# A modelled deadline for VectorE's background work, and 1024-wide products, in an attention and state-space kernel

## The chip, the cores and the metric

One core of a Trainium2 chip. The time is device microseconds (us) of the whole kernel, in the median of repeated executions. PE is the matmul engine (PEld its weight loads), ScalarE (ACT in the records) does exponentials, VectorE (DVE) does everything elementwise here, and SP issues DMA. The times of one kernel on one chip spread by 0.08% to 0.25%, mostly about 1 us.

## The reference, cut to what matters

The kernel computes two things from the same `x` (2048 x 1024) and mixes them with a gate:

```python
a = state_space(x)     # Bu = x @ B_bar; h[t] = Lam_bar * h[t-1] + Bu[t] (complex, 1024 states); y = 2 Re(h @ C) + x * Dskip
b = attention(x)       # 32 heads of 32, 2048 x 2048 scores per head, softmax, @ wo
g = sigmoid((x * gate_w).sum(-1))
out = g * a + (1 - g) * b
```

The softmax needs 32 x 2048 x 2048 exponentials, which is 1,024 tiles of 128 x 1024. Everything else is arranged around them.

## The kernel before: the parts that matter

The program is a fixed order of 512 *bursts*. A burst puts score matmuls for two tiles into PSUM (4 x 2 `qk` pairs), has both tiles exponentiated, multiplies exponentials of earlier bursts, mostly two or three ago, with V (`pv`, in "quarters"), and adds about four *dense* matmuls of 512 columns from a list: projections (`proj`, `vproj`), state inputs (`u`), output maps (`c`), the output projection (`out`). Dense matmuls all use one PSUM bank, so VectorE must evacuate the bank before the next dense group starts.

The two exponentials of a burst normally both run on ScalarE. In 52 listed bursts VectorE makes half of the first tile with a polynomial, and ScalarE only the other half:

```python
def dve_bursts():
    out = []
    for lo, hi, m in ((172, 188, 4), (204, 254, 4), (296, 332, 4), (400, 508, 4)):
        out += [B for B in range(lo, hi) if B % m == 1 and B != 457]
    return out
DVB = set(dve_bursts())
...
    # in exp(B, z, s)
    if z == 0 and B in DVB:
        self.dve_exp(B, s, p)       # ScalarE 128x512, VectorE 128x512 in one PSUM pass and four SBUF passes
    else:
        self.act(lambda e: e.activation(self.tile[p], ps[:, 2 * s:2 * s + 2, :], ACT.Exp, scale=SCALE), ...)
```

VectorE's queue is filled at build time. Between evacuations the builder places *background*: tables, folded maps, and for each of 32 state tiles the rotation, scan and rotation back. The old rule used one constant period per burst:

```python
PERIOD = 1.81 ; DPERIOD = 1.40          # us per burst, without and with VectorE's help
...
early = 0.1 + 0.1 * len(tail) + (0.2 if used < base else 0.0)
limit = t0 + (period - early if ended is not None else period + (0.3 if p + 1 in DVB else PE_HEAD))
while not self.dx and (self.bg or self.bg2):
    ...
    if c > 0 and st + c > limit:
        break
    src.pop(0)[1]()                     # the op goes into VectorE's queue here
```

The background of a state tile (real and imaginary part, each 128 x 512 bf16) had eight narrow products:

```python
tt(0.335, t[0], ure, er, ALU.mult, ...)      # and three more, then two adds into fp32
...                                          # two scans
tt(0.335, t[0], hre, er, ALU.mult, ...)      # and three more, then two adds
```

Of the kernel before, what the change touches and what calls it, by code (L numbers as in the profile page):

```python
# [12 lines left out]
ALU = mybir.AluOpType  # L13
# [912 lines left out]
QUNITS = 8  # L926
BURSTS = 8
NBURST = GROUPS * QUNITS * BURSTS
PERIOD = 1.81
PE_HEAD = 0.86  # L930
MM_PER_PERIOD = 4
DPERIOD = 1.40
EXP_A = 16713.9646930418
EXP_B = 4936176.0
EXP_C2 = 189883.03836007958
# [11 lines left out]
DVB = set(dve_bursts())  # L947
# [17 lines left out]
class FastPath:  # L965
# [86 lines left out]
    def dve(self, fn, r, w, name=""):  # L1052
        return self.S.op("dve", fn, reads=r, writes=w, name=name)
# [271 lines left out]
    def table_ops(self, j):  # L1325

        EF, Et, prod = self.EF, self.Et, self.fold.rearrange("p (k a b) -> p k a b", k=4, a=32)
        lo = [EF[:, r, 16 * j:16 * (j + 1)].unsqueeze(1).to_broadcast([128, 32, 16]) for r in range(2)]
        hi = [EF[:, r, 128 + 32 * j:160 + 32 * j].unsqueeze(2).to_broadcast([128, 32, 16]) for r in range(2)]
        first = ["m_a0", "m_a1", "m_a2", "m_k", "m_h", "m_y", "m_s"] if j == 0 else []  # L1330
        over = [("pt", 12 + j // 2), ("pt", 16 + j // 2)]
        ops = []
        for k, (x, y) in enumerate(((0, 0), (1, 1), (0, 1), (1, 0))):
            ops.append((0.62, lambda k=k, x=x, y=y: self.dve(lambda e: e.tensor_tensor(prod[:, k], hi[x], lo[y], ALU.mult), self.EFtok, ["gp%d" % k] + (first if k == 0 else []))))
        for r, op in ((0, ALU.subtract), (1, ALU.add)):
            out = Et[:, r, j, :].rearrange("p (a b) -> p a b", a=32)
            ops.append((0.62, lambda r=r, op=op, out=out: self.dve(lambda e: e.tensor_tensor(out, prod[:, 2 * r], prod[:, 2 * r + 1], op), ["gp%d" % (2 * r), "gp%d" % (2 * r + 1)],
                                                                   [("Et", j)] + (over if r == 0 else []) if r == 0 else [("Et", j)])))
        ops.append((0.0, lambda: self.tabled.append(j)))
        return ops  # L1340

    def item_ops(self, j, ch, n):
        dve, ub, tq, ut, ht = self.dve, self.ub, self.tq, self.ut, self.ht
        b = self.hp_of[ch]
        hp = self.hpb[b]
        er, ei = self.Et[:, 0, j, :], self.Et[:, 1, j, :]
        k = self.ub_of(n)
        ure, uim = ub[k][:, 0, :], ub[k][:, 1, :]
        u0, u1, Et = ("ub", k, 0), ("ub", k, 1), ("Et", j)
        t = [tq[:, i, :] for i in range(4)]  # L1350
        ops = []

        def tt(c, o, a, b, op, r, w):
            ops.append((c, lambda: dve(lambda e: e.tensor_tensor(o, a, b, op), r, w)))  # L1354
        tt(0.335, t[0], ure, er, ALU.mult, [u0, Et], [("tq", 0)])
        tt(0.335, t[1], uim, ei, ALU.mult, [u1, Et], [("tq", 1)])
        tt(0.335, t[2], uim, er, ALU.mult, [u1, Et], [("tq", 2)])
        tt(0.335, t[3], ure, ei, ALU.mult, [u0, Et], [("tq", 3)])
        tt(0.6, ut[:, 0, :], t[0], t[1], ALU.add, [("tq", 0), ("tq", 1)], [("ut", 0)])
        tt(0.6, ut[:, 1, :], t[2], t[3], ALU.subtract, [("tq", 2), ("tq", 3)], [("ut", 1)])  # L1360
        rr = self.pf[:, self.RR, j:j + 1].to_broadcast([128, 512])
        for ri in range(2):
            ops.append((1.29, lambda ri=ri: dve(lambda e: e.tensor_tensor_scan(ht[:, ri, :], rr, ut[:, ri, :], self.init[:, ri, j:j + 1], ALU.mult, ALU.add),  # L1363
                                                [("ut", ri), "init", ("pf", self.RR)], [("ht", ri)])))
        if ch < 3:
            ops.append((0.13, lambda: dve(lambda e: e.tensor_copy(self.hl[:, :, j], ht[:, :, 511]), [("ht", 0), ("ht", 1)], [("hl", j)])))
        hre, him = ht[:, 0, :], ht[:, 1, :]
        tt(0.335, t[0], hre, er, ALU.mult, [("ht", 0), Et], [("tq", 0)])
        tt(0.335, t[1], him, ei, ALU.mult, [("ht", 1), Et], [("tq", 1)])
        tt(0.335, t[2], hre, ei, ALU.mult, [("ht", 0), Et], [("tq", 2)])  # L1370
        tt(0.335, t[3], him, er, ALU.mult, [("ht", 1), Et], [("tq", 3)])
        hw = ["warm"] if ch == 0 and j == 0 else []
        if ch == 2 and j >= 4:
            hw = self.x_toks(0)
        if b == 1 and j == 0:
            hw = ["fX", "fY", "m_c"] + self.EFtok + ["gp%d" % i for i in range(4)]
        tt(0.335, hp[:, 0, j, :], t[0], t[1], ALU.subtract, [("tq", 0), ("tq", 1)], [("hp", b, j, 0)] + hw)
        tt(0.335, hp[:, 1, j, :], t[2], t[3], ALU.add, [("tq", 2), ("tq", 3)], [("hp", b, j, 1)] + hw)
        if j == 7 and ch < 3:
            ops.append((0.0, self.carry))  # L1380
        return ops
# [159 lines left out]
    def plan(self):  # L1541
# [3 lines left out]
        used = {}  # L1545
# [35 lines left out]
        for b in sorted(range(RING), key=lambda b: when.get(b, b)):  # L1581
            p = when.get(b, b)
            ok = [(end, t) for t, end in pairs if free[t] < p and used[b] < end and not (end == NBURST and used[b] >= RING + t[0] // 2)]
            assert ok, (b, p)

            near = [(end, t) for end, t in ok if end - used[b] <= 1]
            end, t = min(near) if near else max(ok)
            free[t] = used[b]
            self.pt_at[b] = t
        self.ring_at, k, x = {}, 2 * RING, 0  # L1590
        for B in range(RING, NBURST):
            for z in range(2):
# [141 lines left out]
    def build(self):  # L1734
# [50 lines left out]
        wo1 = last = False  # L1785
        nal = nc = 0
        self.c_end = 0
        tnext = 0.0
        nq = 0
        log = self.log = []  # L1790
        for p in range(first, NBURST):
# [1 line left out]
            assert not proj[g] or (g == 0 and p < 32)  # L1793
            self.p = p
            second = self.burst(p)
            t0 = tnext
            period = DPERIOD if p in DVB else PERIOD
            tnext = t0 + period
            if p in DVB:
                self.dve_t = max(self.dve_t, t0 + 0.35) + 0.70  # L1800
            nq += len(self.quarters[p])
            ends = nq % 32 == 0 and self.quarters[p]
            ntail = 0
            if p % 2 and not ends:
                ntail = 1 if p in DVB else 2 if p + 2 in DVB else 0
            head, tail = self.split_pv(p, ntail)
            self.pv(head)
            second()
            if ends:
                self.normalize(nq // 32 - 1)  # L1810
                self.dve_t = max(self.dve_t, t0 + PE_HEAD) + 0.75
            if p >= C_LOADS and p % 4 == 0 and nc < 8:
                self.ld_c(nc)
                nc += 1
# [23 lines left out]
            if g >= 6 and not cs and self.c_left[3] == 0 and nal < 8 and p > self.c_end:  # L1838
                self.ld_a(nal)
                nal += 1  # L1840
            used = 0.0
            quota = 3 if p in DVB else 5 if p + 1 in DVB and not 442 <= p < 459 and (cur is None or cur.left >= 8) else MM_PER_PERIOD
            base = quota
            ended = None
            while used < quota:
# [31 lines left out]
                wt, f = cur.pieces.pop(0)  # L1877
                f()
                used += wt
                cur.left -= wt  # L1880
                if not cur.pieces:
                    ended = cur
# [1 line left out]
                elif used >= quota and cur.left <= 1 and quota == base:  # L1884
                    quota += 1
            self.pv(tail)
            log.append((p, ended.tag if ended else (cur.tag if cur else None), used, round(self.dve_t - t0, 2), len(self.bg) + len(self.bg2)))
            early = 0.1 + 0.1 * len(tail) + (0.2 if used < base else 0.0)
            limit = t0 + (period - early if ended is not None else period + (0.3 if p + 1 in DVB else PE_HEAD))
            while self.dx:  # L1890
                c, fn = self.dx[0]
                st = max(self.dve_t, t0)
                if st + c > limit:
                    break
                self.dx.pop(0)
                fn()
                self.dve_t = st + c
            while not self.dx and (self.bg or self.bg2):
                src = self.bg if self.bg and (self.bg[0][2] in self.tabled or not self.bg2) else self.bg2
                if not src:  # L1900
                    break
                c = src[0][0]
                st = max(self.dve_t, t0 + 0.3)
                if c > 0 and st + c > limit:
                    break
                src.pop(0)[1]()
                if c > 0:
                    self.dve_t = st + c
            if getattr(self, "seen_items", 0) != self.items_done:
                self.seen_items = self.items_done  # L1910
                self.item_p = p
            if ended is not None:
                ended.evac()
                self.dve_t = max(self.dve_t, t0 + period - early + 0.1) + 0.70 + ended.extra
        self.log = log
        assert not outs and cur is None and nq == 4 * NBURST - 8
        self.tail()

    def tail(self):

# [178 lines left out]
```

## Time and profile before

| | before |
|---|---|
| median of 4 runs | 940.23 us (939.22 to 940.47) |
| ScalarE / PE / VectorE busy | 98% / 99% / 72% |
| first exponential ends / last ends / end of span | 11.00 / 929.70 / 939.17 us |

The first part of the profile page, busy time of each engine with its share of the span and its instructions:

```profile
span 939.2 us, 33706 instructions
...
PE 925.4 (99%) x15316; PEld 520.3 (55%) x15316; DVE 674.1 (72%) x1357; ACT 923.2 (98%) x1034; POOL 10.0 (1%) x39
```

Two engines look full. The chain of waits that ended last, by engine, even names PE first:

```profile
PE 61%; ACT 36%; SPq 1%; DMA 1%; issue 0%; DVE 0%; DVEq 0%
```

The Trainium skill, "Perfetto Trace Analysis", section "Identifying the Most-Contended Engine", warns that a matmul engine's busy share is no good measure of how close it is to its limit, because matmuls are pipelined, while for ScalarE and VectorE the occupancy is a fair one. This trace agrees: PE's 99% includes 57.6 us that its weight loads stood waiting for ScalarE, hidden under matmuls whose ends are modelled. The list of waits (who waited for whom, us in total, times, longest):

```profile
PEld f_ps L1635 <- ACT f_pt L1651: 57.6, 143, 0.6
DVE f_ub L1452 <- PE f_ps L1446: 40.4, 47, 3.0
DVE f_Ag L1488 <- PE f_ps L1475: 18.4, 32, 1.8
```

The second line shows what the change is after: VectorE stood idle in front of 47 of the 48 evacuations of state inputs that go to `ub` (16 more go to another tile). The old rule let the background run only to 0.1 to 0.5 us before the burst's booked end.

The table by stretches of time (start and end, length, then busy us and instructions of each engine, PE's granted clock, DMA share, GB/s):

```profile
core 0: us, PE busy (x) PEld busy (x) DVE busy (x) ACT busy (x) POOL busy (x), PEclk, DMA share, GB/s
100.00:200.00 100.00, 99.92 (x1662) 54.42 (x1659) 86.69 (x174) 100.00 (x111) 1.68 (x6) 1.00 0.37 68
300.00:400.00 100.00, 99.90 (x1665) 56.82 (x1664) 69.67 (x141) 100.00 (x114) 1.51 (x6) 1.00 0.12 30
927.50:930.50 3.00, 3.00 (x39) 1.65 (x38) 1.80 (x4) 2.20 (x3) 0.00 (x0) 0.50 0.11 37
```

ScalarE is busy 100.00 of 100 us, but PE is at 99.9 too, so this table alone does not say which of them sets the time. ScalarE's busy time cannot show small stalls, though, because consecutive records overlap. So I took the *ends* of consecutive ScalarE instructions from the trace: 903 of 1,033 are 0.915 to 0.920 us apart, and the end of a half-wide one follows after 0.490 us. What these distances have beyond 0.9165 or 0.4905 us, summed from the end of the first exponential to the end of the last, is called the **stall sum** below; three small instructions in between are taken out with their own time. Before: 2.99 us of 918.7.

The groups of the narrow products (count, then shortest/median/longest duration in ns, first and last start):

```profile
L1354 DVE TENSOR_TENSOR f_tq<-f_ht,f_Et x128: 398/418/426, 63.6 to 725.8; 128x512 bf16<-128x512 bf16 x128
L1354 DVE TENSOR_TENSOR f_tq<-f_ub,f_Et x96: 415/418/424, 53.7 to 718.0; 128x512 bf16<-128x512 bf16 x96
```

They last 0.418 us but follow each other every 0.334 us in the trace: the record of one overlaps the next.

### The profile page before, as it was taken

The numbers are of one execution on the slowest core, as the hardware profiler recorded it, in microseconds if no ns is written. First come the engines' busy times: TensorE is split into PE (matmuls) and PEld (weight loads), VectorE is DVE, ScalarE is ACT, GpSimd is POOL, SyncE is SP. The second block draws the span as 40 slices with busy tenths as digits, with TensorE's granted clock in tenths as the row PEclk, the third lists the DMA queues.
The fourth block names the chain that finished last, engine by engine and source line by source line (L and its number), as shares of the span: only waits on it lengthen the run. The fifth ranks groups of instructions, "written<-read, shape, count | busy, mean of one in ns | idle before, by whom it ended". The sixth has DMA issues, their size and how long they took to land.

```text
span 939.2 us, 33706 instructions
## 1 busy us (share of the span) xinstructions
PE 925.4 (99%) x15316; PEld 520.3 (55%) x15316; DVE 674.1 (72%) x1357; ACT 923.2 (98%) x1034; POOL 10.0 (1%) x39
## 2 busy tenths in 40 slices
PE   8999999999999999999999999999999999999996
PEld 4555645565555565555655755544655556555553
DVE  2688888888888766657688766568838466676775
ACT  6999999999999999999999999999999999999996
POOL 2000000000000000000000000000000000000000
PEclk9999999999999999999999999999999999999998
DMA  9659433310133002121023301142201212233412
GB/s 202 104 93 146 76 56 80 74 31 27 34 66 89 30 6 52 41 72 31 19 42 61 75 16 42 42 94 53 53 5 40 73 52 79 80 87 122 115 62 74
DMA packets 157076, 60.90 MB, mean 65 GB/s; under 512 B 145664, under 2 KB 145664, under 8 KB 156928
## 3 DMA queue, kind: packets, MB, share of 16 engines
q1 hardware_dynamic: 154768, 58.16, 28.0%
q8 instruction: 121, 1.98, 0.9%
q10 hardware_dynamic: 2160, 0.53, 0.3%
q14 instruction: 27, 0.22, 0.1%
HBM read 16.79 MB, written 12.58 MB: 31 GB/s over the span
## 4 chain that ended last, share of the span: by engine, by line
PE 61%; ACT 36%; SPq 1%; DMA 1%; issue 0%; DVE 0%; DVEq 0%
ACT f_pt L1651 33%; PE f_ps L1703 17%; PE f_ps L1635 13%; PE f_ps L1446 9%; PE f_ps L1475 9%; PE f_ps L1416 8%; PE f_ps L1434 4%; ACT f_ub L1671 1%; SPq L1068 1%; ACT f_cT_re L1651 1%; DMA f_xT<-in_A_x_dram 1%; ACT f_Et L1651 1%; ACT f_cT_im L1651 1%; PE f_ps L1481 1%; ACT f_OT L1651 0%
## 5 line engine op out<-in xcount | busy, mean ns | idle before, releaser
L1651 ACT ACTIVATE f_pt<-f_ps 128x1024 bf16<-128x1024 f32 x892 | 834.0, 1277 | 0.6 <-PE f_ps L1635 0.6
L1703 PEld LDWEIGHTS f_ps<-f_V,f_pt 128*128 128x128 bf16 x7136 | 228.4, 96 | 115.9 <-issue 94.1
L1703 PE MATMUL f_ps<-f_V,f_pt 128*128 128x33 bf16 x7136 | 279.6, 178 | 0.0
L1635 PE MATMUL f_ps<-f_Q,f_K 32*128 32x256 bf16 x4096 | 230.3, 273 | 3.8 <-ACT f_cT_re L1651 1.2
L1635 PEld LDWEIGHTS f_ps<-f_Q,f_K 32*128 32x128 bf16 x4096 | 80.3, 92 | 158.5 <-issue 73.0
L1446 PE MATMUL f_ps<-f_xT,f_wb 128*128 128x512 bf16 x512 | 131.0, 377 | 0.3
L1416 PE MATMUL f_ps<-f_xT,f_wb 128*128 128x512 bf16 x464 | 119.0, 378 | 0.0
L1363 DVE TENSOR_TENSOR_SCAN f_ht<-f_pf,f_init,f_ut 128x512 bf16<-128x512 f32 x64 | 80.4, 1272 | 0.0
L1475 PE MATMUL f_ps<-f_cT_re,f_hp 128*128 128x512 bf16 x192 | 72.6, 378 | 0.1
L1475 PE MATMUL f_ps<-f_cT_im,f_hp 128*128 128x512 bf16 x192 | 72.6, 378 | 0.0
L1506 PE MATMUL f_ps<-f_wb,f_OT 128*128 128x512 bf16 x252 | 65.7, 379 | 0.1
L1452 DVE CAST f_ub<-f_ps 128x512 bf16<-128x512 f32 x48 | 33.2, 692 | 40.4 <-PE f_ps L1446 40.4
L1434 PE MATMUL f_ps<-f_wb,f_xT 128*128 128x128 bf16 x896 | 59.2, 219 | 0.0
L1446 PEld LDWEIGHTS f_ps<-f_xT,f_wb 128*128 128x128 bf16 x512 | 40.4, 96 | 32.0
L1416 PEld LDWEIGHTS f_ps<-f_xT,f_wb 128*128 128x128 bf16 x464 | 36.3, 96 | 28.0
L1434 PEld LDWEIGHTS f_ps<-f_wb,f_xT 128*128 128x128 bf16 x896 | 50.4, 97 | 0.0
L1672 DVE TENSOR_SCALAR f_ut<-f_ps 128x512 int32<-128x512 f32 x26 | 18.0, 692 | 39.9 <-PE f_ps L1635 39.9
L1354 DVE TENSOR_TENSOR f_tq<-f_ht,f_Et 128x512 bf16<-128x512 bf16 x128 | 45.9, 417 | 0.0
L1354 DVE TENSOR_TENSOR f_ut<-f_tq 128x512 f32<-128x512 bf16 x64 | 42.1, 683 | 0.0
L1488 DVE TENSOR_SCALAR f_Ag<-f_ps,f_gcol 128x512 f32<-128x512 f32 x32 | 24.0, 751 | 18.4 <-PE f_ps L1475 18.4
L1354 DVE TENSOR_TENSOR f_tq<-f_ub,f_Et 128x512 bf16<-128x512 bf16 x96 | 34.6, 417 | 0.0
L1423 DVE CAST f_Q<-f_ps 128x512 bf16<-128x512 f32 x30 | 20.8, 692 | 15.9 <-PE f_ps L1416 15.8
(152 smaller groups left out, 853.6 us busy)
## 6 DMA issues: line engine op xcount, KB each, us to landing
ag_scratch<-f_Ag SPq DMA_DIRECT2D x32, 256.0 KB, 2.5
f_hp<-ag_scratch SPq DMA_DIRECT2D x32, 256.0 KB, 2.9
f_wb<-in_B_wqkv_dram SPq DMA_DIRECT2D x21, 256.0 KB, 4.3
out_dram<-f_xT SPq DMA_DIRECT2D x16, 256.0 KB, 2.1
f_wb<-in_B_wo_dram SPq DMA_DIRECT2D x1, 1024.0 KB, 5.2
f_OT<-f_On SPq DMA_TRANSPOSE x63, 2.3
f_wb<-in_B_wo_dram SPq DMA_DIRECT2D x1, 768.0 KB
f_wb<-in_B_wqkv_dram ACTq DMA_DIRECT2D x2, 256.0 KB, 4.2
```

The costliest lines, as they stand in the source:

```text
L1354: ops.append((c, lambda: dve(lambda e: e.tensor_tensor(o, a, b, op), r, w)))
L1363: ops.append((1.29, lambda ri=ri: dve(lambda e: e.tensor_tensor_scan(ht[:, ri, :], rr, ut[:, ri, :], self.init[:, ri, j:j + 1], ALU.mult, ...
L1416: mms.append((1, lambda e, f, l, a=a: e.matmul(ps[:, bank, :], w[:, g % 2, part, a, :], xT[:, a, 512 * ch:512 * (ch + 1)], start=f, stop=l ...
L1434: m = e.matmul(ps[:, bank, 128 * q:128 * (q + 1)], xT[:, a, 128 * kt:128 * (kt + 1)], w[:, g % 2, 2, a, :], start=(a == 0), stop=(a == 7))
L1446: mms.append((1, lambda e, f, l, a=a: e.matmul(ps[:, 7, :], bT[:, n % 2, ri, a, :], xT[:, a, 512 * ch:512 * (ch + 1)], start=f, stop=l), [ ...
L1452: self.dve(lambda e: e.tensor_copy(self.ub[k][:, ri, :], ps[:, 7, :]), [("bank", 7)], [("ub", k, ri)] + over, "evac_u")
L1475: mms.append((1, lambda e, f, l, j=j, ri=ri: e.matmul(ps[:, 7, :], hp[:, ri, j, cols], cT[ri][:, j, 512 * cb:512 * (cb + 1)], start=f, sto ...
L1488: self.dve(lambda e: e.tensor_scalar(a, ps[:, 7, :], self.gcol[:, 0, tt:tt + 1], None, ALU.mult), [("bank", 7), "g0"], [at], "evac_c")
L1506: mms.append((1, lambda e, f, l, j=j: e.matmul(ps[:, 7, :], OT[:, j, 256 * qb + 128 * r:256 * qb + 128 * (r + 1)], wo[j][0][:, 512 * cb:51 ...
L1635: m = e.matmul(ps[:, 2 * sl[z] + h % 2, 256 * kl:256 * (kl + 1)], K[32 * h:32 * h + 32, g % 2, 128 * kt:128 * (kt + 1)], Q[32 * h:32 * h + ...
L1651: self.act(lambda e: e.activation(self.tile[p], ps[:, 2 * s:2 * s + 2, :], ACT.Exp, scale=SCALE), [("S", s)], [("pt", p)], "exp")
L1703: m = e.matmul(ps[:, 6, o:o + 33], self.tile[p][:, h2, 256 * kl + 128 * qt:256 * kl + 128 * (qt + 1)], V[:, g % 2, 2 * i + kl, h, :], star ...
```

## The change

Its intent: fill VectorE's idle time before evacuations without making them late, and make the background shorter. The diff, cut to its core:

```diff
-PERIOD = 1.81
-PE_HEAD = 0.86
+ACT_2 = 0.9165          # full exponential, also ACT_1 = 0.49, lags, and
+QK_PE = 0.34            # PE's time for scores; PV_PE = 0.101 per quarter, MM_PE = 0.2157 per dense matmul
...
-        tt(0.335, t[0], ure, er, ALU.mult, [u0, Et], [("tq", 0)])
-        tt(0.335, t[1], uim, ei, ALU.mult, [u1, Et], [("tq", 1)])
-        tt(0.335, t[2], uim, er, ALU.mult, [u1, Et], [("tq", 2)])
-        tt(0.335, t[3], ure, ei, ALU.mult, [u0, Et], [("tq", 3)])
+        E2, E2r = self.Et[:, :, j, :], self.Et[:, ::-1, j, :]       # both table halves; the same in reversed order
+        tt(0.602, tq[:, 0:2, :], ub[k], E2, ALU.mult, [u0, u1, Et], [("tq", 0)])
+        tt(0.602, tq[:, 2:4, :], ub[k], E2r, ALU.mult, [u0, u1, Et], [("tq", 2)])
...                                                  (the same for ht)
-        tnext = 0.0
+        self.T = self.act_t = self.evac_t = 0.0
...
-                ntail = 1 if p in DVB else 2 if p + 2 in DVB else 0
+            ntail = 2 if p % 2 and not ends else 0      # PV quarters behind the dense matmuls in odd bursts
...
+            a0 = max(self.act_t, T + QK_LAG) + (ACT_1 if isd else ACT_2)
+            self.act_t = a0 + ACT_2
+            self.T = max(ta, tp)                        # the next burst starts when ScalarE frees a tile and PE is done
+            if ended is not None:                       # a dense group ended: leave room for its evacuation
+                cost = 0.608 if ended.tag in ("proj", "vproj", "u") else 0.668
+                nxt_dense = self.T + QK_PE + PV_PE * len(self.quarters.get(p + 1, ()))
+                self.fill(max(ready, nxt_dense - cost - 0.15))
+            else:
+                self.fill(self.T + (QK_LAG if p + 1 in DVB else 1.0))
```

The 512 bursts, their exponentials, the list of VectorE's half exponentials and the matmuls stay.

More of the change, by code (lines that the diff above doesn't have):

```diff
@@ L928 @@
 NBURST = GROUPS * QUNITS * BURSTS
-PERIOD = 1.81
-PE_HEAD = 0.86
+ACT_2 = 0.9165
+ACT_1 = 0.49
+ACT_LAG = 0.466
+QK_LAG = 0.449
+QK_PE = 0.34
+PV_PE = 0.101
+MM_PE = 0.2157
 MM_PER_PERIOD = 4
-DPERIOD = 1.40
 EXP_A = 16713.9646930418
@@ L1331, in table_ops @@
         over = [("pt", 12 + j // 2), ("pt", 16 + j // 2)]
+        after = 1 + max(self.tile_end.get(t, 0) for t in (12 + j // 2, 16 + j // 2))
         ops = []
         for k, (x, y) in enumerate(((0, 0), (1, 1), (0, 1), (1, 0))):
-            ops.append((0.62, lambda k=k, x=x, y=y: self.dve(lambda e: e.tensor_tensor(prod[:, k], hi[x], lo[y], ALU.mult), self.EFtok, ["gp%d" % k] + (first if k == 0 else []))))
+            ops.append((0.6, lambda k=k, x=x, y=y: self.dve(lambda e: e.tensor_tensor(prod[:, k], hi[x], lo[y], ALU.mult), self.EFtok, ["gp%d" % k] + (first if k == 0 else []))))
         for r, op in ((0, ALU.subtract), (1, ALU.add)):
             out = Et[:, r, j, :].rearrange("p (a b) -> p a b", a=32)
-            ops.append((0.62, lambda r=r, op=op, out=out: self.dve(lambda e: e.tensor_tensor(out, prod[:, 2 * r], prod[:, 2 * r + 1], op), ["gp%d" % (2 * r), "gp%d" % (2 * r + 1)],
-                                                                   [("Et", j)] + (over if r == 0 else []) if r == 0 else [("Et", j)])))
+            ops.append((0.6, lambda r=r, op=op, out=out: self.dve(lambda e: e.tensor_tensor(out, prod[:, 2 * r], prod[:, 2 * r + 1], op), ["gp%d" % (2 * r), "gp%d" % (2 * r + 1)],
+                                                                   [("Et", j)] + (over if r == 0 else []) if r == 0 else [("Et", j)]), after))
         ops.append((0.0, lambda: self.tabled.append(j)))
@@ L1354, in tt @@
             ops.append((c, lambda: dve(lambda e: e.tensor_tensor(o, a, b, op), r, w)))
-        tt(0.335, t[0], ure, er, ALU.mult, [u0, Et], [("tq", 0)])
-        tt(0.335, t[1], uim, ei, ALU.mult, [u1, Et], [("tq", 1)])
-        tt(0.335, t[2], uim, er, ALU.mult, [u1, Et], [("tq", 2)])
-        tt(0.335, t[3], ure, ei, ALU.mult, [u0, Et], [("tq", 3)])
-        tt(0.6, ut[:, 0, :], t[0], t[1], ALU.add, [("tq", 0), ("tq", 1)], [("ut", 0)])
-        tt(0.6, ut[:, 1, :], t[2], t[3], ALU.subtract, [("tq", 2), ("tq", 3)], [("ut", 1)])
+        E2, E2r = self.Et[:, :, j, :], self.Et[:, ::-1, j, :]
+        tt(0.602, tq[:, 0:2, :], ub[k], E2, ALU.mult, [u0, u1, Et], [("tq", 0)])
+        tt(0.602, tq[:, 2:4, :], ub[k], E2r, ALU.mult, [u0, u1, Et], [("tq", 2)])
+        tt(0.6, ut[:, 0, :], t[0], t[1], ALU.add, [("tq", 0)], [("ut", 0)])
+        tt(0.6, ut[:, 1, :], t[3], t[2], ALU.subtract, [("tq", 2)], [("ut", 1)])
         rr = self.pf[:, self.RR, j:j + 1].to_broadcast([128, 512])
         for ri in range(2):
-            ops.append((1.29, lambda ri=ri: dve(lambda e: e.tensor_tensor_scan(ht[:, ri, :], rr, ut[:, ri, :], self.init[:, ri, j:j + 1], ALU.mult, ALU.add),
+            ops.append((1.192, lambda ri=ri: dve(lambda e: e.tensor_tensor_scan(ht[:, ri, :], rr, ut[:, ri, :], self.init[:, ri, j:j + 1], ALU.mult, ALU.add),
                                                 [("ut", ri), "init", ("pf", self.RR)], [("ht", ri)])))
         if ch < 3:
-            ops.append((0.13, lambda: dve(lambda e: e.tensor_copy(self.hl[:, :, j], ht[:, :, 511]), [("ht", 0), ("ht", 1)], [("hl", j)])))
-        hre, him = ht[:, 0, :], ht[:, 1, :]
-        tt(0.335, t[0], hre, er, ALU.mult, [("ht", 0), Et], [("tq", 0)])
-        tt(0.335, t[1], him, ei, ALU.mult, [("ht", 1), Et], [("tq", 1)])
-        tt(0.335, t[2], hre, ei, ALU.mult, [("ht", 0), Et], [("tq", 2)])
-        tt(0.335, t[3], him, er, ALU.mult, [("ht", 1), Et], [("tq", 3)])
+            ops.append((0.19, lambda: dve(lambda e: e.tensor_copy(self.hl[:, :, j], ht[:, :, 511]), [("ht", 0), ("ht", 1)], [("hl", j)])))
+        tt(0.602, tq[:, 0:2, :], ht[:], E2, ALU.mult, [("ht", 0), ("ht", 1), Et], [("tq", 0)])
+        tt(0.602, tq[:, 2:4, :], ht[:], E2r, ALU.mult, [("ht", 0), ("ht", 1), Et], [("tq", 2)])
         hw = ["warm"] if ch == 0 and j == 0 else []
@@ L1376, in item_ops @@
             hw = ["fX", "fY", "m_c"] + self.EFtok + ["gp%d" % i for i in range(4)]
-        tt(0.335, hp[:, 0, j, :], t[0], t[1], ALU.subtract, [("tq", 0), ("tq", 1)], [("hp", b, j, 0)] + hw)
-        tt(0.335, hp[:, 1, j, :], t[2], t[3], ALU.add, [("tq", 2), ("tq", 3)], [("hp", b, j, 1)] + hw)
+        tt(0.335, hp[:, 0, j, :], t[0], t[1], ALU.subtract, [("tq", 0)], [("hp", b, j, 0)] + hw)
+        tt(0.335, hp[:, 1, j, :], t[2], t[3], ALU.add, [("tq", 2)], [("hp", b, j, 1)] + hw)
         if j == 7 and ch < 3:
@@ L1589, in plan @@
             self.pt_at[b] = t
+        self.tile_end = {t: e for pr, e in free.items() for t in pr}
         self.ring_at, k, x = {}, 2 * RING, 0
@@ L1795, in build @@
             second = self.burst(p)
-            t0 = tnext
-            period = DPERIOD if p in DVB else PERIOD
-            tnext = t0 + period
-            if p in DVB:
-                self.dve_t = max(self.dve_t, t0 + 0.35) + 0.70
+            T = self.T
+            isd = p in DVB
+            a0 = max(self.act_t, T + QK_LAG) + (ACT_1 if isd else ACT_2)
+            self.act_t = a0 + ACT_2
+            ta = a0 + ACT_LAG
+            if isd:
+                self.dve_t = max(self.dve_t, T + QK_LAG) + 0.608
+                ta = max(ta, self.dve_t + 0.19)
             nq += len(self.quarters[p])
             ends = nq % 32 == 0 and self.quarters[p]
-            ntail = 0
-            if p % 2 and not ends:
-                ntail = 1 if p in DVB else 2 if p + 2 in DVB else 0
+            ntail = 2 if p % 2 and not ends else 0
+            if isd:
+                ntail = min(ntail, 1)
             head, tail = self.split_pv(p, ntail)
@@ L1808, in build @@
             second()
+            pe = T + QK_PE + PV_PE * len(head)
             if ends:
+                rn = pe + 0.35
+                self.fill(rn)
                 self.normalize(nq // 32 - 1)
-                self.dve_t = max(self.dve_t, t0 + PE_HEAD) + 0.75
+                self.dve_t = max(self.dve_t, rn) + 0.6
             if p >= C_LOADS and p % 4 == 0 and nc < 8:
@@ L1841, in build @@
             used = 0.0
+            if cur is None:
+                pe = max(pe, self.evac_t)
             quota = 3 if p in DVB else 5 if p + 1 in DVB and not 442 <= p < 459 and (cur is None or cur.left >= 8) else MM_PER_PERIOD
@@ L1879, in build @@
                 used += wt
+                pe += MM_PE if wt else 0.055
                 cur.left -= wt
@@ L1886, in build @@
             self.pv(tail)
-            log.append((p, ended.tag if ended else (cur.tag if cur else None), used, round(self.dve_t - t0, 2), len(self.bg) + len(self.bg2)))
-            early = 0.1 + 0.1 * len(tail) + (0.2 if used < base else 0.0)
-            limit = t0 + (period - early if ended is not None else period + (0.3 if p + 1 in DVB else PE_HEAD))
-            while self.dx:
-                c, fn = self.dx[0]
-                st = max(self.dve_t, t0)
-                if st + c > limit:
-                    break
-                self.dx.pop(0)
-                fn()
-                self.dve_t = st + c
-            while not self.dx and (self.bg or self.bg2):
-                src = self.bg if self.bg and (self.bg[0][2] in self.tabled or not self.bg2) else self.bg2
-                if not src:
-                    break
-                c = src[0][0]
-                st = max(self.dve_t, t0 + 0.3)
-                if c > 0 and st + c > limit:
-                    break
-                src.pop(0)[1]()
-                if c > 0:
-                    self.dve_t = st + c
+            ready = pe + 0.2
+            tp = pe + PV_PE * len(tail) + 0.1
+            self.T = max(ta, tp)
+            log.append((p, ended.tag if ended else (cur.tag if cur else None), used, round(self.T - T, 3), round(self.dve_t - T, 2), len(self.bg) + len(self.bg2), round(self.T, 2), round(tp - T, 3)))
+            if ended is not None:
[4 more added lines that the diff above has]
+                self.fill(self.T + (QK_LAG if p + 1 in DVB else 1.0))
             if getattr(self, "seen_items", 0) != self.items_done:
@@ L1913, in build @@
                 ended.evac()
-                self.dve_t = max(self.dve_t, t0 + period - early + 0.1) + 0.70 + ended.extra
+                st = max(self.dve_t, ready)
+                self.evac_t = st + cost + 0.13
+                self.dve_t = st + cost + ended.extra
         self.log = log
@@ L1917, in build, with fill @@
         self.tail()
+    def fill(self, limit):
+        while True:
+            for src in (self.dx, self.bg, self.bg2):
+                if not src:
+                    continue
+                if src is self.bg:
+                    n = src[0][2]
+                    if n < 8 and n not in self.tabled or n >= 8 and len(self.folded) < 16:
+                        continue
+                if src is self.bg2 and len(src[0]) > 2 and self.p < src[0][2]:
+                    continue
+                c = src[0][0]
+                if c == 0 or self.dve_t + c <= limit:
+                    src.pop(0)[1]()
+                    self.dve_t += c
+                    break
+            else:
+                return
     def tail(self):
```

## The prediction

> **What bounds the kernel now.** ScalarE's exponentials. The table by stretches of time shows ScalarE busy 100.00 of every 100 us from 50 us to 900 us. In the trace, the ends of consecutive 128x1024 exponentials are 0.916 to 0.918 us apart in 850 of 1,033 cases, and 0.490 us after a half-wide one. 972 full and 52 half instructions make 972 x 0.9165 + 52 x 0.4905 = 916.3 us. The first exponential ends at 11.0 us and the last at 929.7 us, so 918.7 us hold 916.3 us of work: the stalls of ScalarE in the whole middle are about 2.4 us. They are crumbs of 0.02 to 0.13 us: at 60 to 118 us (bursts where PE itself needs over 1.83 us) and around 413-430, 575-612 and 757-793 us (bursts where VectorE takes half an exponential). In front stand 11 us of head, behind 9.5 us of tail. It agrees with the Trainium skill, "ScalarE: Activation LUTs", which states one element per cycle and lane whatever the function (0.833 ns per element): 1024 of them are 0.853 us of the measured 0.917.
>
> PE's 99% includes modelled ends; in the list of waits its score matmuls wait 57.6 us for ScalarE. VectorE is 72% busy.
>
> **What the change does.** (1) Eight 512-wide bf16 products per state tile become four 1024-wide ones. Back-to-back ends in the trace: 0.334 us for 512 wide bf16, 0.601 us for the same count with fp32 output, which is about 0.068 us fixed plus 0.52 or 1.04 ns per element. So a 1024-wide bf16 product is an estimated 0.60 us against 0.668 us for two; 128 pairs give 8.7 us, provided the reversed order of the two table halves keeps the fast mode. The Trainium skill, "VectorE: DVE Perf Modes", asks for 16-bit and step one, which the inner dimension keeps; this case's 0.334 against 0.601 us agrees with its factor of two. (2) A new rule fills VectorE's queue with background up to a modelled deadline. Its durations equal the trace's (1.19 scan, 0.60, 0.9165). (3) Two of a burst's PV quarters move behind its dense matmuls in nearly every odd burst, which gives evacuations 0.2 us more. (4) State projections and output chunks come some bursts earlier or later. The 512 bursts, the exponentials, VectorE's share of them, PE's total work, head and tail stay.
>
> **On the critical path:** almost nothing. VectorE's 8.7 us were not on it. Only stalls can change: at best -2.4 us, realistically -0.5 to -1. Against that, VectorE runs closer to its deadlines; a late evacuation delays the next dense group, and past some tenths of a us ScalarE stalls.
>
> **Prediction:** 939.3 us, 8 in 10 between 937.5 and 942.0. Faster by over 2%: 0.01; within 2%: 0.97; slower by over 2%: 0.02.
>
> **What would show it.** VectorE's busy time falls from 674 to about 665 us; the product line shows 64+48+16 instructions of 128x1024, spaced 0.60 us; ScalarE still 100 of 100 us in each stretch; its end-to-end spacing still 0.917 us; summed stalls between first and last exponential between 1.5 and 4 us; the last exponential ends near 928-931 us, with the same 9.5 us behind it.
>
> **What would make it wrong.** A reversed outer step that loses the fast mode (about 1.13 us per op, 64 ops, +34 us of VectorE and a model that no longer holds, so repeated late evacuations); background put in front of evacuations in many bursts; or moved PV quarters holding tiles that the next exponential overwrites.

## The result, and the profile after

| | before | after |
|---|---|---|
| median of 4 runs each | 940.23 us | 940.29 us (939.77 to 940.92) |
| ratio, 95% interval | | 1.0003, 0.9986 to 1.002: the same |
| stall sum | 2.99 us | 3.07 us |
| first exponential's end to last one's | 918.70 us | 918.78 us |

Ratios here are the mean time of one kernel's fast runs over the mean of the other's in the same rounds, so not quite the ratio of the quoted medians.

The first part of the page, and the list of waits, after:

```profile
span 938.2 us, 33573 instructions
...
PE 923.3 (98%) x15316; PEld 532.7 (57%) x15316; DVE 659.5 (70%) x1229; ACT 923.0 (98%) x1034; POOL 11.3 (1%) x39
```

```profile
PEld f_ps L1637 <- ACT f_pt L1653: 42.8, 104, 0.6
DVE f_ub L1453 <- PE f_ps L1447: 24.1, 25, 3.0
DVE f_Ag L1489 <- PE f_ps L1476: 39.5, 29, 6.6
```

The change does on VectorE what it was meant to do: 128 instructions fewer, 14.6 us less busy, and idle time in front of 25 of 48 evacuations of state inputs into `ub` instead of 47. The idle time did not vanish, though, but moved to other evacuations: in front of those of the output maps (`Ag`) it grew from 18.4 to 39.5 us. The new order did this, not the shorter products, since it is 49.0 us in `order_only` below and 19.6 us in `wide_only`. The groups of the wide products:

```profile
L1359 DVE TENSOR_TENSOR f_tq<-f_ht,f_Et x64: 679/684/692, 59.2 to 720.8; 128x1024 bf16<-128x1024 bf16 x64
L1359 DVE TENSOR_TENSOR f_tq<-f_ub,f_Et x48: 678/684/693, 52.4 to 714.9; 128x1024 bf16<-128x1024 bf16 x48
```

All lie within 0.678 to 0.693 us, so the half of them that read the table with a reversed outer step run as fast as the others. One directly behind another, they end 0.600 to 0.607 us apart (47 cases, median 0.602), against twice 0.334.

And nothing of it reaches the time. The table by stretches:

```profile
core 0: us, PE busy (x) PEld busy (x) DVE busy (x) ACT busy (x) POOL busy (x), PEclk, DMA share, GB/s
100.00:200.00 100.00, 100.00 (x1635) 55.91 (x1631) 91.00 (x170) 100.00 (x110) 2.04 (x6) 1.00 0.38 70
300.00:400.00 100.00, 99.98 (x1670) 58.45 (x1669) 52.17 (x96) 100.00 (x114) 0.00 (x0) 1.00 0.12 30
927.50:930.50 3.00, 2.66 (x59) 1.82 (x53) 2.21 (x8) 2.42 (x3) 0.00 (x0) 1.00 0.25 92
```

From 300 to 400 us VectorE has 17.5 us less to do (the second chunk's state tiles are written by 287 us instead of 327), and ScalarE is at 100.00 of 100 as before.

A trap lies in the last row. The profiled span fell by 1.0 us, from 939.2 to 938.2. But from 927.5 to 930.5 us the run before was granted half the PE clock (0.50), the run after the full one, and the tail behind the last exponential took 9.47 us in one and 8.24 us in the other. The stretch between first and last exponential is equal to 0.1 us. Of the 1.23 us between the tails, 0.96 had arisen by the start of the first reciprocal behind the last exponential (1.42 us after its end in one run, 0.46 in the other). The medians of the runs agree with the stretch, not with the span; the profiled execution of before (940.91 us) is not among the four runs of the table and lies above all of them.

The stall sum stayed because one part fell and another rose. In the stretch 560 to 620 us it fell from 0.81 to about 0.5 us. From 40 to 60 us, where there had been less than 0.03 us, there are now 0.68 us, most of it one stall. ScalarE's timeline there, first before, then after (start, duration, instruction; in brackets idle time and what ended it):

```profile
43.30 2.23 ACT L1651 ACTIVATE f_pt<-f_ps 128x1024 bf16<-128x1024 f32 x2
45.20 1.25 ACT L1651 ACTIVATE f_cT_re<-f_ps 128x1024 bf16<-128x1024 f32 x1
```

```profile
43.30 2.13 ACT L1653 ACTIVATE f_pt<-f_ps 128x1024 bf16<-128x1024 f32 x2
45.78 1.02 ACT L1653 ACTIVATE f_cT_re<-f_ps 128x1024 bf16<-128x1024 f32 x1 [0.34 <-PE f_ps L1637]
```

What led to it, from the same timeline of after, VectorE and PE:

```profile
42.42 0.55 DVE L1283 SCALAR_TENSOR_TENSOR f_OT<-f_OT 128x384 f32<-128x384 f32 x1
43.01 0.36 DVE L1284 TENSOR_SCALAR f_OT<-f_OT 128x384 f32<-128x384 f32 x1
...
43.29 0.23 DVE L1243 TENSOR_TENSOR f_pf<-f_pf,f_W 128x8 f32<-128x8 f32 x2
43.48 0.17 DVE L1244 TENSOR_SCALAR f_pf<-f_pf 128x8 f32<-128x8 f32 x1
43.56 0.68 DVE L1453 CAST f_ub<-f_ps 128x512 bf16<-128x512 f32 x1
...
44.39 1.02 PE L1447 MATMUL f_ps<-f_xT,f_wb 128*128 128x512 bf16 x4 [0.66 <-DVE f_pf L1243]
```

The evacuation (L1453) stands behind table and parameter work in VectorE's queue; the dense matmuls (L1447) wait 0.66 us for it, the scores behind them come late, and ScalarE runs dry. The releaser is printed as `f_pf L1243`, the VectorE instruction nearest to the semaphore event; what PE needed was the evacuation just before it. The timing model starts with VectorE idle at burst 16 (38.5 us in this trace). The trace shows VectorE busy at that point with work placed earlier, until about 40.7 us.

### The profile page after: what moved, and what is told of

It is laid out like the page before. It is cut to its first block, busy times and chain, and to the rows that moved or that the text cites. A ratio compares the mean times of both kernels' runs of the same rounds, so it can differ in the third digit from the quotient of the medians.

```text
span 938.2 us, 33573 instructions
## 1 busy us (share of the span) xinstructions
PE 923.3 (98%) x15316; PEld 532.7 (57%) x15316; DVE 659.5 (70%) x1229; ACT 923.0 (98%) x1034; POOL 11.3 (1%) x39
## 3 DMA queue, kind: packets, MB, share of 16 engines
q8 instruction: 121, 1.98, 0.9%
## 4 chain that ended last, share of the span: by engine, by line
PE 60%; ACT 37%; DVE 1%; DMA 1%; issue 0%; DVEq 0%; SPq 0%
ACT f_pt L1653 34%; PE f_ps L1705 17%; PE f_ps L1637 13%; PE f_ps L1447 9%; PE f_ps L1476 9%; PE f_ps L1417 8%; PE f_ps L1435 4%; ACT f_ub L1673 1%; DMA f_xT<-in_A_x_dram 1%; ACT f_OT L1653 1%; ACT f_cT_re L1653 1%; ACT f_Et L1653 1%; PE f_ps L1482 1%; ACT f_cT_im L1653 0%; PE f_ps L1142 0%
## 5 line engine op out<-in xcount | busy, mean ns | idle before, releaser
L1705 PEld LDWEIGHTS f_ps<-f_V,f_pt 128*128 128x128 bf16 x7136 | 241.4, 96 | 133.8 <-issue 97.1
L1705 PE MATMUL f_ps<-f_V,f_pt 128*128 128x33 bf16 x7136 | 294.0, 178 | 0.2 <-ACT f_pt L1653 0.2
L1637 PE MATMUL f_ps<-f_Q,f_K 32*128 32x256 bf16 x4096 | 234.2, 273 | 3.8 <-ACT f_pt L1653 1.2
L1637 PEld LDWEIGHTS f_ps<-f_Q,f_K 32*128 32x128 bf16 x4096 | 82.4, 92 | 125.3 <-issue 53.3
L1447 PE MATMUL f_ps<-f_xT,f_wb 128*128 128x512 bf16 x512 | 131.0, 377 | 0.8 <-DVE f_pf L1243 0.7
L1447 PEld LDWEIGHTS f_ps<-f_xT,f_wb 128*128 128x128 bf16 x512 | 40.2, 96 | 32.0 <-issue 0.7
L1489 DVE TENSOR_SCALAR f_Ag<-f_ps,f_gcol 128x512 f32<-128x512 f32 x32 | 24.0, 751 | 39.7 <-PE f_ps L1476 39.5
L1453 DVE CAST f_ub<-f_ps 128x512 bf16<-128x512 f32 x48 | 33.0, 688 | 24.4 <-PE f_ps L1447 24.1
L1359 DVE TENSOR_TENSOR f_tq<-f_ht,f_Et 128x1024 bf16<-128x1024 bf16 x64 | 42.0, 684 | 0.2
L1674 DVE TENSOR_SCALAR f_hp<-f_ps 128x512 int32<-128x512 f32 x17 | 11.8, 691 | 34.4 <-PE f_ps L1637 34.4
```

The lines of the kernel that those rows point to most:

```text
L1359: ops.append((c, lambda: dve(lambda e: e.tensor_tensor(o, a, b, op), r, w)))
L1447: mms.append((1, lambda e, f, l, a=a: e.matmul(ps[:, 7, :], bT[:, n % 2, ri, a, :], xT[:, a, 512 * ch:512 * (ch + 1)], start=f, stop=l), [ ...
L1453: self.dve(lambda e: e.tensor_copy(self.ub[k][:, ri, :], ps[:, 7, :]), [("bank", 7)], [("ub", k, ri)] + over, "evac_u")
L1637: m = e.matmul(ps[:, 2 * sl[z] + h % 2, 256 * kl:256 * (kl + 1)], K[32 * h:32 * h + 32, g % 2, 128 * kt:128 * (kt + 1)], Q[32 * h:32 * h + ...
L1674: self.S.op("dve", lambda e: e.tensor_scalar(xi, ps[:, 2 * s + 1, :], EXP_A, EXP_B, ALU.mult, ALU.add), reads=[("S", s)], writes=[("xi", k ...
L1705: m = e.matmul(ps[:, 6, o:o + 33], self.tile[p][:, h2, 256 * kl + 128 * qt:256 * kl + 128 * (qt + 1)], V[:, g % 2, 2 * i + kl, h, :], star ...
```

## The experiments

Theories. **S**: ScalarE's exponentials set the time; VectorE and PE matter only through stalls of some tenths of a us. Rivals: **P**, PE sets the time, as its busy share and the chain suggest. **G**, wide products and order each change the time, and cancel. The runs came on three chips; each is compared with runs of the kernel before on its own chip, whose medians were 939.66, 939.62 and 940.03 us.

| run | median us (runs) | ratio to before, 95% interval | VectorE busy us | stall sum us |
|---|---|---|---|---|
| wide_only | 939.63 (5) | 1.0001, 0.9987 to 1.0015 | 666.4 | 2.70 |
| order_only | 940.45 (5) | 1.0006, 0.9992 to 1.0020 | 666.9 | 3.65 |
| less_pe | 939.08 (4) | 0.9991, 0.9976 to 1.0006 | 660.3 | 1.98 |
| more_dve | 943.35 (4) | 1.0041, 1.0026 to 1.0057 | 742.9 | 6.71 |
| no_help | 961.21 (4) | 1.0228, 1.0213 to 1.0244 | 501.1 | 1.95 |
| more_help | 934.97 (5) | 0.9949, 0.9935 to 0.9962 | 705.6 | 3.95 |
| more_help_old | 938.61 (5) | 0.9987, 0.9974 to 1.0001 | 686.8 | 4.39 |
| more_help_late | 933.93 (5) | 0.9936, 0.9923 to 0.9950 | 705.3 | 3.01 |
| late_start | 939.24 (5) | 0.9994, 0.9980 to 1.0007 | 659.4 | 2.85 |
| nine_old | 937.77 (5) | 0.9978, 0.9965 to 0.9992 | 702.4 | 4.44 |
| nine_new | 937.34 (5) | 0.9968, 0.9955 to 0.9982 | 687.4 | 4.77 |
| more_help_narrow | 936.22 (5) | 0.9956, 0.9943 to 0.9970 | 713.1 | 4.61 |

A stall sum comes from one profiled execution. In its first 40 us, where these kernels are alike, it varies between 0.1 and 1.1 us from run to run; I read single stretches behind that, and trust sums to no better than 1 us.

### The two halves of the change alone

`wide_only` is the kernel before with the wide products, booked at 0.67 us each (the price of two narrow ones), so that the old order stays. `order_only` is the changed kernel with the narrow products.

```diff
 # wide_only, on the kernel before             # order_only: the reverse edit, on the changed kernel
-tt(0.335, t[0], ure, er, ...) and three more
+tt(0.67, tq[:, 0:2, :], ub[k], E2, ...)
+tt(0.67, tq[:, 2:4, :], ub[k], E2r, ...)
```

> The kernel before with the 1024-wide products alone; its old scheduler books 0.67 us for each, as for two narrow ones, so the order of the queue stays. Theory S (ScalarE's exponentials set the time): 939 to 941 us, VectorE busy about 665 us instead of 674, stalls of ScalarE between its first and last exponential 2.5 to 3.5 us. Rival G (each part of the change acts, and they cancel): the wide products alone gain 3 to 8 us, so 932 to 937 us.

> The changed kernel with narrow products, so the new order alone. Theory S: 939 to 941 us, VectorE busy about 668 us or more. Rival G: the new order alone loses 3 to 8 us, so 943 to 948 us.

Both are the same as before within 0.2%; G falls. VectorE's busy time fell by 7.7 us with the wide products, near the estimated 8.7. It also fell by 7.2 us with the order alone, where no work was saved. That is no gain but a matter of reading: busy time counts overlapping records once, and the new order lets more operations follow each other directly, where 0.418 us records stand 0.334 us apart. Adding up the lengths of all VectorE records shows it: 735.6 us before, 734.6 in `order_only`, 716.4 in `wide_only`.

### PE lighter

```diff
-mms.append((1, lambda e, f, l, j=j, ri=ri: e.matmul(ps[:, 7, :], hp[:, ri, j, cols], cT[ri][:, j, 512 * cb:512 * (cb + 1)], ...
+n = 512 if (j, ri) in ((0, 0), (7, 1)) else 128
+mms.append((1, lambda e, f, l, j=j, ri=ri, n=n: e.matmul(ps[:, 7, 0:n], hp[:, ri, j, cols], cT[ri][:, j, 512 * cb:512 * cb + n], ...
```

> The changed kernel with 448 of the 512 output-map matmuls cut from 512 to 128 columns (the result is wrong on purpose): an estimated 448 x 0.16 = 72 us of PE work gone, nothing else. Theory S: 937 to 940 us. Rival P (PE, 98% busy and 60% of the chain of waits, sets the time): 870 to 900 us.

The result is wrong (relative error 0.025). The first part of its page, and the wait of the score matmuls' weights for ScalarE:

```profile
PE 886.8 (95%) x15316; PEld 528.0 (56%) x15316; DVE 660.3 (70%) x1229; ACT 921.9 (98%) x1034; POOL 11.3 (1%) x39
```

```profile
PEld f_ps L1638 <- ACT f_pt L1654: 83.9, 176, 0.7
```

PE's busy time fell by 36.5 us and not by the estimated 72 (probably because its records overlap; the granted clock was also a little lower, 0.991 against 0.997), its weight loads waited 83.9 us for ScalarE instead of 42.8, and the stretch from the first to the last exponential's end fell by 1.1 us against the changed kernel (917.69 to 918.78). P expected 870 to 900 us and falls. The times do not resolve this gain (the interval includes 1), but the trace says where the small stalls came from: those at 400 to 430, 580 to 620 and 740 to 800 us, where bursts with VectorE's help fall together with output maps, are gone, so there PE's work in a shortened burst was the cause. The stalls from 40 to 120 us, before the first output map, stayed as they were.

### ScalarE heavier

```diff
-DVB = set(dve_bursts())
+DVB = set()
```

> The changed kernel with all 52 half exponentials given back from VectorE to ScalarE. Theory S: 52 x (0.9165 - 0.4905) = 22.2 us more, so 959 to 964 us. Rival P (PE sets the time, its work is the same): 938 to 942 us.

The first part of its page:

```profile
PE 925.5 (97%) x15095; PEld 544.7 (57%) x15316; DVE 501.1 (52%) x969; ACT 944.1 (98%) x1034; POOL 11.3 (1%) x39
```

961.21 us against 939.62 of the kernel before on the same chip is 21.6 us more. The stretch between the exponentials took 939.81 us against 918.78, so 21.0 us more: 52 x 0.426 = 22.2 us, less the 1.1 us by which the stall sum fell. VectorE lost 158 us of work and it bought nothing. (PE's 15,095 recorded matmuls against 15,316 weight loads are records that this trace lacks, not fewer matmuls.) S holds at the size it expected.

### VectorE heavier

```diff
 tt(0.602, tq[:, 0:2, :], ub[k], E2, ALU.mult, [u0, u1, Et], [("tq", 0)])
+tt(0.602, tq[:, 0:2, :], ub[k], E2, ALU.mult, [u0, u1, Et], [("tq", 0)])      # and so for all four
```

> The changed kernel with each of the 128 wide products done twice, into the same place: 128 x 0.60 = 77 us more VectorE work, which its timing model is told. Theory S: 939 to 942 us with VectorE busy about 735 us. A rival in which VectorE's load matters: 960 us or more.

The first part of its page, and two of its waits:

```profile
PE 920.9 (98%) x15316; PEld 528.4 (56%) x15316; DVE 742.9 (79%) x1357; ACT 925.6 (98%) x1034; POOL 9.5 (1%) x39
```

```profile
PE f_ps L1451 <- DVE f_Ag L1493: 1.1, 3, 0.4
PE f_ps L1451 <- DVE f_K L1428: 1.1, 4, 0.3
```

943.35 us: 1.35 us above the range that I had given to S. The 83.4 us of added busy time lengthened the stretch between the exponentials by 3.6 us (922.42 against 918.78), all of it stall sum, in new crumbs of 0.10 to 0.38 us over most of the run. So VectorE is off the critical path only as a sum. Each operation more before an evacuation uses up some of the distance to PE, and beyond it ScalarE pays: between 60 and 920 us PE's matmuls wait for VectorE 16 times here, 4.4 us in all (the two lines are part of it), and not once in the changed kernel. About 4% of the added work came through. My expectation was wrong in taking the order's model for exact. It books the added work, and PE still waited; which delays it leaves out was not traced.

### VectorE's room turned into fewer exponentials on ScalarE

If S is right, the room that the change makes is worth something only when VectorE takes work from ScalarE.

```diff
 # more_help, on the changed kernel
-DVB = set(dve_bursts())
+DVB = set(dve_bursts()) | {165, 169, 189, 193, 197, 201, 289, 293, 457} | set(range(333, 354, 4))
 # more_help_old, on the kernel before
+DVB = set(dve_bursts()) | {189, 193, 197, 201}
 # more_help_late, on more_help; late_start has this line alone
         self.T = self.act_t = self.evac_t = 0.0
+        self.dve_t = 2.1
```

> The changed kernel with 15 more half exponentials on VectorE (67 instead of 52), which the new order has room for. Theory S: 15 x 0.426 = 6.4 us less at best, with some stalls 934 to 936 us. Rival P: 939 to 941 us.

> The kernel before with 4 more half exponentials (56), bursts 189 to 201, as many as I found that its old order takes there; with 6 or more its build stops at its own assertion that a state tile is done in time. Theory S: 4 x 0.426 = 1.7 us less, so 938 to 939 us.

> As more_help, and the timing model starts with VectorE 2.1 us behind instead of idle, as the trace shows it at that point. Theory S: the stall of 0.45 us at 46 us goes, so 0.3 to 0.7 us less than more_help: 933.5 to 935.5 us.

`more_help` ran in 934.97 us, `more_help_late` in 933.93 us, and their runs do not overlap (934.22 to 935.70 against 933.48 to 934.21). This beats the kernel before, by 0.64% at the best, and so the changed kernel, which is the same as it. The sum works out: from the first exponential's end to the last one's, `more_help_late` took 912.33 us and the changed kernel 918.78 us, which is 6.45 us less; 15 x 0.426 = 6.4 us were expected, and the stall sums are equal (3.01 and 3.07 us). Its first part of the page:

```profile
PE 900.3 (97%) x15095; PEld 529.7 (57%) x15316; DVE 705.3 (76%) x1304; ACT 916.7 (98%) x1034; POOL 11.1 (1%) x39
```

`more_help_old` gained 1.0 us of the 1.7; its ratio's interval just includes 1.

> The changed kernel whose timing model starts with VectorE 2.1 us behind instead of idle. Theory S: the stalls of ScalarE between its first and last exponential fall from 3.07 us to 2.2 to 2.6 us, the time by 0.4 to 0.9 us, which lies near the spread of the runs: 939 to 940 us. Rival: the stall at 46 us is VectorE's work itself and only moves, so the sum stays at 3.0 us or more.

With the model's start moved, the stretch from 40 to 60 us, which held 0.68 us of stalls, holds less than 0.08 us. ScalarE's timeline there, to be compared with the one of after above:

```profile
43.54 2.13 ACT L1653 ACTIVATE f_pt<-f_ps 128x1024 bf16<-128x1024 f32 x2
45.35 1.24 ACT L1653 ACTIVATE f_cT_re<-f_ps 128x1024 bf16<-128x1024 f32 x1
```

The next exponential starts while the one in front is still recorded, with no idle time. So the stall was a wrong starting value of the model and not VectorE's load. The whole stall sum fell only to 2.85 us and missed the expected 2.2 to 2.6, because this one execution had 0.78 us of stalls in its first 40 us, where the edit changes nothing; behind 40 us it is 2.07 against 2.97 us. The time (939.24 us, interval including 1) does not resolve it. Between `more_help` and `more_help_late`, which differ by the same line, the medians differ by 1.0 us.

### What made the room

I had written that 4 more was all I found for the old order. That was too hasty: placed otherwise it takes 9. With burst 349, 293 or 457 more, or 165 and 169 beside 189 to 201, its build stops at its own assertions (state tiles, output projections, or the polynomial of the help before, not done in time). The changed kernel builds with all 15, and so does the new order with narrow products.

An obvious rival is that the wide products would make the same room in the old order. It was not run, but it was built: with the wide products booked at 0.602 us the old order stops too, with all 15 and with each tenth burst beside the nine. Of the 15, 12 build singly in the old order and 11 in the old order with wide products; no ten of these build together in either.

```diff
 # nine_old on the kernel before, nine_new on the changed kernel
+DVB = set(dve_bursts()) | {169, 189, 193, 197, 201} | set(range(333, 346, 4))
 # more_help_narrow: order_only with the 15 bursts and dve_t = 2.1
```

> Corrects an expectation on record: the old order takes more than 4 extra half exponentials, if they are placed otherwise; 9 is the most that I found to build (bursts 169, 189 to 201, 333 to 345). Theory S: 9 x 0.426 = 3.8 us less, with new stalls 936 to 937.5 us.

> The same 9 extra half exponentials in the changed kernel. Theory S alone: as nine_old, 936 to 937.5 us. If the new order also stalls ScalarE less under this load: 0.5 to 1.5 us less than nine_old.

> more_help_late with narrow products: which part of the change makes the room for 15 more. If the order makes it: within 1 us of more_help_late's 933.9 us. If the wide products make it: stalls of ScalarE grow from 3.0 to 6 us or more, 937 us or more.

Nine more gave 2.3 us in the old order and 2.7 us in the new one, of 3.8 booked; `nine_old` came out 0.3 us above its expected range. The medians of the two differ by 0.4 us, the means by 0.7, and the runs overlap (937.64 to 938.67 against 936.80 to 937.70), so the 0.5 us and more that I had asked for are not settled by the time. (`nine_new` is the whole change, wide products included. It has the start stall that `late_start` removes, and 1.05 us of stalls in its first 40 us.) Behind 60 us, where neither matters, the stalls are 4.05 us in `nine_old` and 3.04 in `nine_new`. What the order gives besides is that six more can be built at all.

The narrow products with all 15 came to 936.22 us on another chip; by the ratios, 0.9956 against 0.9936, that is 0.2% or about 1.9 us more than `more_help_late`, though the intervals overlap a little. Its stall sum is 4.61 against 3.01 us, of which 0.6 us lie in the first 40 us, where the two kernels are alike. That lies between what the two explanations expected. The other 1.0 us comes with the narrow products: most of it lies from 740 to 800 us, where both runs of the new order with narrow products (`order_only` and this one) have 1.02 us of stalls, and those with wide products, done once, 0.41 us or less. So the order (with all that belongs to it, the moved PV quarters too) makes the room, and the wide products save about 1 us of stalls under this load. How much of the 1.9 us of time is real stays open.

## Why the prediction was right

- **The time.** 939.3 us were predicted, 940.29 measured, inside 937.5 to 942.0, and "within 2%" with a chance of 0.97 came true. The reason was the right one: `no_help` moved the time by what ScalarE was given, `less_pe` and the wide products did not move it.
- **VectorE's products.** 0.60 us estimated for a 1024-wide product, 0.600 to 0.607 measured back to back, the reversed ones included. The 8.7 us were 7.7 in `wide_only`.
- **VectorE's busy time.** About 665 us predicted, 659.5 measured. The step that was off: the prediction subtracted saved work only. The busy share also falls when the same work stands closer together, by 7.2 us in `order_only`.
- **The stalls before.** "About 2.4 us" was mis-sized: the sum took all 916.3 us of exponentials from a stretch that starts at the *end* of the first one and so holds one fewer. Counted right it is 3.3 us, of which the three small instructions take 0.3 and stalls 2.99 us.
- **The gain.** "Realistically -0.5 to -1" did not come; +0.06 us was measured. With an interval of about -1.3 to +1.9 us the time alone could not have shown so small a gain; the stalls behind the first 40 us, 2.97 us against 2.65, say that it is not there. It was part of the predicted 939.3, and the range was wide enough to do without it. Stalls around 590 us fell by 0.3 us, and one new place at 46 us cost 0.68 us, because the model starts with an idle VectorE. The prediction had named the mechanism (a late evacuation delays the next dense group), without seeing that it would occur once, at a wrong starting value.
- **The tail.** "The same 9.5 us behind it" held for work, not for this record: 8.24 us. The profiled execution of before had PE at half clock for 3 us there.
- **Not tested.** What the moved PV quarters alone do was not run. Their risk, tiles held too long, shows nowhere: ScalarE's stalls from 120 to 400 us sum to 0.04 us, against 0.05 before.

## What to carry to other kernels

Two engines can both look full, as ScalarE and PE did here at 99.9 to 100 of 100 us; which one sets the time was told by taking work from one and giving work to the other (`less_pe`, `no_help`). Where that shows one engine, an improvement on another was worth nothing by itself in this case; ask what work of the full engine the freed time can take, and change both together (here 15 half exponentials, 6 us). A build-time model of several engines may be very good and still cost at its edges: check its starting values against the trace. And compare the stretch that the change touches rather than the spans of two single profiles, since half a PE clock for 3 us in a tail was as large as all that was looked for.

## What the Trainium skill lacked or had wrong

- "VectorE: DVE Perf Modes", section "The TRN2 errata", gives `58 + FD/Accel` cycles of 0.96 GHz for VectorE from SBUF and says that it under-predicts the duration of a single operation. Here both figures hold, for different things: 512 wide at two per cycle gives 0.327 us by the row, and back-to-back operations are 0.334 us apart, while each one's record lasts 0.418 us. This section does not say that the row fits the spacing; the page of the next point does keep the two apart.
- "Perfetto Trace Analysis", section "Optimizing Scalar/DVE Operations", states about 125 ns of overhead per VectorE operation on PSUM and about 51 ns per ScalarE operation on PSUM. It calls these engine-busy times, so they are to be compared with the spacing. Here evacuating casts of 128 x 512 fp32 from PSUM end 0.600 us after the operation before them (after, median of the 46 that stand directly behind one), which at one element per cycle of 0.96 GHz leaves 67 ns, as from SBUF. ScalarE's full and half exponentials, 0.9165 and 0.4905 us apart, differ by 0.426 us for 512 elements and leave 64 ns.
- The two-source product with a reversed *outer* step (both halves of a table in reverse) keeps the two-per-cycle rate: 0.678 to 0.693 us a record, as without. "Vector Engine (DVE) Microarchitecture Reference", section "Performance modes", lists operands with a negative step among what was not measured.
